# A weight conversion's shifted word in PSUM, and the conversions placed 300 instead of 1000 priorities late

## The chip, the core and the metric

The kernel runs on one core of a Trainium2 chip. The metric is the device time of one execution, in microseconds; lower is better. Engines are named TensorE (PE, with its weight loads PEld), VectorE (DVE), ScalarE (ACT), GpSimd (POOL) and SyncE (SP, whose queue issues the DMAs).

## What is computed

Attention with a top-32 mask (4 batches, 8 heads, 576 tokens, head size 64), then a feed-forward net on the 2304 tokens, then a mixture of 8 experts of which each token takes 2.

```
scores = q @ k.T / sqrt(D);  keep the 32 largest of each row;  attn = softmax;  x = attn @ v
h = maximum(x @ w_in, 0);  x = (h * h) @ w_out            # 512 -> 2048 -> 512
top2 of x @ w_gate + log1p(exp(x @ w_noise)) * noise       # routing
out[token] += weight * (maximum(x @ w1[e], 0) @ w2[e])     # 512 -> 1024 -> 512, per expert
```

The FFN's weights can arrive as 64-bit floats. They are turned into two 32-bit parts on the chip (a rounded high part and the rest), so that products can be made of three TensorE passes: high by high, high by low, low by high.

## The kernel before

Attention goes in 80 units: a unit is a pair of heads of one batch for 128 query rows, or the pair's last 64 rows. A full unit has two searches of 128x576 scores, a unit of last rows one, 144 in all. A search runs on VectorE (`scores`, lines 351 to 384): in six segments of 96 the 8 largest are taken and struck out (L367, L368), the 8 largest of what is left are taken over the row (L369, once per search, so its count shows the progress), and four more rounds run over the candidates (L372, L374). Then `softmax` (L386 to L397) works on ScalarE and GpSimd, TensorE transposes (`transpose4`, `rest`) and multiplies with V (`times_v`), and `finish` splits the result into the FFN's input xT.

The first batch's 16 units (12 full ones and 4 of last rows, 28 searches) hold the three token tiles of FFN chunk 0. The loop over the units (L731 to L762) emits the scores of a unit two units ahead (`AHEAD`). The FFN (`ffn`, L265) works on chunks of three tiles of 128 tokens and 16 slices f of its weights. For each slice, 12 matmuls into a tile `pf` (L286 to L288), ScalarE and GpSimd steps on it, and 9 matmuls (L272 to L274) into three accumulators `acc`, which are held from the first slice of a chunk to its last. The accumulators come from the pool `ps_acc`, three PSUM banks. The FFN's pieces are emitted between attention's, as filling work, through `step`.

The order on every engine is set by a planner: it takes the instructions by priority (a higher number is later, and each instruction emitted adds to it) among those that are ready in its own model of time, and within an engine the order it finds is fixed. `FILL_LATER = 350` gives the FFN's filling work a priority 350 later than where it is emitted; `side` (L640) does the same for the conversions and for the zero fill of the output buffers (`ZEROS_LATER = 1500`). Two conversions are emitted at the end of each unit until all 32 are out, that is by the end of the 16th unit. A tile is taken from its pool in the order in which the tiles are asked for, so the conversions stand ahead of the FFN.

One conversion (`convert`, L140) loads 512 KB (`raw`, three buffers), and on words of 128x512: ScalarE scales the high words into `ca` (L148), VectorE shifts `ca` by three bits (L149) and combines it with the sign bit of the high words (L150), ScalarE scales the low words (L151), GpSimd adds (L152), ScalarE rounds to the high part (L155), GpSimd subtracts (L156), and SP stores the two parts to `wsc` in DRAM (L157), from where the FFN loads them. The PSUM has 8 banks: `pf` 1, `acc` 3, the scores 2, attention's other tiles 2.

Of the kernel before, what the change touches and what calls it, by code (L numbers as in the profile page):

```python
# [8 lines left out]
F32 = mybir.dt.float32  # L9
F32R = mybir.dt.float32r  # L10
I32 = mybir.dt.int32
U32 = mybir.dt.uint32
BF16 = mybir.dt.bfloat16
AF = mybir.ActivationFunctionType
ALU = mybir.AluOpType
PSUM = bass.MemoryType.PSUM

P = 128
# [16 lines left out]
EARLY = 2  # L35
SOON = 300
FILL_LATER = 350
CONVERT_LATER = 1000
ZEROS_LATER = 1500


# [11 lines left out]
def attention_ffn_moe(ctx: ExitStack, tc: tile.TileContext, q, k, v, w_ffn, w_route, noise, w_exp, out,  # L53
# [3 lines left out]
    nc = tc.nc  # L57
    B, H, S, D = SHAPE
    NT, DM = out.shape
# [44 lines left out]
    for t, (b, i) in enumerate(tiles):  # L104
        if i == 0:
            nc.gpsimd.iota(tok_i[:, t:t + NFULL], pattern=[[P, NFULL]], base=b * S, channel_multiplier=1)
        elif i is None:
            nc.gpsimd.iota(tok_i[:, t:t + 1], pattern=[[0, 1]], base=b * S + NFULL * P, channel_multiplier=1)
            nc.gpsimd.tensor_scalar(tok_i[LEFT:P, t:t + 1], tok_i[LEFT:P, t:t + 1], 1.0, float(S - LEFT),
                                    op0=ALU.mult, op1=ALU.add)  # L110
# [7 lines left out]
    ps_acc = wctx.enter_context(tc.tile_pool(name="ps_acc", bufs=3, space=PSUM))  # L118
# [21 lines left out]
    def convert(vpool, f, which):  # L140
        n = DM
        raw = vpool.tile([P, 2 * n], U32, name="raw", bufs=3 if keep is not None else 2)
        nc.sync.dma_start(raw, w_ffn[f, which])
        pair = raw.rearrange("p (j t) -> p j t", t=2)
        lo_w, hi_w = pair[:, :, 0], pair[:, :, 1]
        a = vpool.tile([P, n], U32, name="ca", bufs=2)

        nc.scalar.activation(a.bitcast(F32), hi_w.bitcast(F32), AF.Copy, scale=2.0 ** -112)  # L148
        nc.vector.tensor_scalar(a, a, 3, None, op0=ALU.logical_shift_left)  # L149
        nc.vector.scalar_tensor_tensor(a, hi_w, 0x80000000, a, op0=ALU.bitwise_and, op1=ALU.bitwise_or)  # L150
        nc.scalar.activation(lo_w, lo_w, AF.Copy, scale=2.0 ** -29)  # L151
        nc.gpsimd.tensor_tensor(a, a, lo_w, op=ALU.add)  # L152
        val = a.bitcast(F32)
        sp = vpool.tile([P, 2, n], F32R, name="csp", bufs=2 if keep is not None else 1)
        nc.scalar.activation(sp[:, 0, :], val, AF.Copy)  # L155
        nc.gpsimd.tensor_tensor(sp[:, 1, :], val, sp[:, 0, :].bitcast(F32), op=ALU.subtract)  # L156
        nc.sync.dma_start(wsc[f][:, which], sp.bitcast(F32))  # L157
# [482 lines left out]
    def side(work, n, offset):  # L640
        at = tc.cur_priority
        tc.cur_priority = at + offset
        for _ in range(n):
            next(work, None)
        tc.cur_priority = at
# [4 lines left out]
    def conversions():  # L650
        for f in range(NF):
            for which in range(2):
                convert(vpool, f, which)
                yield
# [76 lines left out]
    for i in range(NU):  # L731
        credit = rate(i)

        def fill(part):
            step(credit * part)
# [24 lines left out]
        fill(FILLS[7])  # L760
        side(convs, CONVERTS, CONVERT_LATER)
        side(zeros, 1, ZEROS_LATER)  # L762
# [34 lines left out]
    for e in range(E):  # L797
        nc.vector.tensor_scalar(over[:, e:e + 1], base[:, e:e + 1], float(-(e * NT + CAP)), 0.0,
                                op0=ALU.add, op1=ALU.max)
# [180 lines left out]
```

## Time and profile before

| | us |
|---|---|
| median of 3 runs (1410.55 to 1411.21) | 1410.84 |
| the profiled execution | 1400.43 |
| its span | 1398.7 |
| TensorE busy in it | 1256.0 |
| VectorE busy in it | 954.0 |
| ScalarE busy in it | 842.5 |
| GpSimd busy in it | 798.0 |

The rows below come from that one profiled execution. Times are microseconds from the start of its span unless a column says ns. A busy share is the time in which an engine worked on an instruction; an instruction that stands and waits for a resource of the memory inside the engine counts as busy.

### The profile page before, as it was taken

Reading aid. Unit: us, or ns where it says so; the run is one execution under the profiler, and the core shown is the slowest. Engines: PE = TensorE matmul, PEld = TensorE weight load, DVE = VectorE, ACT = ScalarE, POOL = GpSimd, SP = SyncE. Lnnn points to the kernel's source line nnn. Section 1 sums busy time; section 2 is a strip of 40 time slices with the busy share of each in tenths; the row PEclk is TensorE's granted clock in tenths of the full one; section 3 lists DMA queues with packets and bytes.
Section 4 is the critical chain, followed back from the end, with each engine's and each line's share of the span. In section 5 each row is a group of like instructions: output and inputs, shape, how many; then the busy total and the mean of one; then the engine's idle time right before and its main releaser. Section 6 shows DMA issues by size and latency. Waiting matters only on the chain.

```text
span 1398.7 us, 26415 instructions
## 1 busy us (share of the span) xinstructions
PE 1256.0 (90%) x7937; PEld 1084.3 (78%) x7937; DVE 954.0 (68%) x5089; ACT 842.5 (60%) x1741; POOL 798.0 (57%) x1366
## 2 busy tenths in 40 slices
PE   2576659998999999999999999899899999999996
PEld 1354447877788888878878888788788999989995
DVE  8999999999989998899998001145554434444342
ACT  5768778978888787888878434354443333233321
POOL 4869898996888675868748523605233405134131
PEclk9877559999999999999999999999999999999998
DMA  9984557973367445546514776737664335444241
GB/s 332 350 306 151 181 179 244 343 235 116 133 207 243 146 141 188 178 144 202 182 65 153 246 248 211 265 106 235 200 210 142 130 114 165 125 143 134 91 145 38
DMA packets 85241, 257.50 MB, mean 184 GB/s; under 512 B 10716, under 2 KB 10844, under 8 KB 85088
## 3 DMA queue, kind: packets, MB, share of 16 engines
q1 hardware_dynamic: 75808, 227.32, 49.0%
q0 software_dynamic: 9280, 28.40, 5.6%
q8 instruction: 65, 1.06, 0.3%
q14 instruction: 88, 0.72, 0.1%
HBM read 205.71 MB, written 52.06 MB: 184 GB/s over the span
## 4 chain that ended last, share of the span: by engine, by line
PE 50%; DVE 31%; DMA 6%; ACT 5%; POOL 4%; issue 3%; SPq 0%; POOLq 0%; DVEq 0%; ACTq 0%
DVE w L368 9%; DVE m L367 6%; PE ph L573 5%; PE ph L572 5%; PE ph L574 5%; PE acc L555 5%; PE acc L553 5%; PE acc L554 5%; DVE m L369 4%; DVE cand L374 4%; DVE m L372 3%; PE acc L274 2%; PE acc L272 2%; PE acc L273 2%; PE pa L445 2%
## 5 line engine op out<-in xcount | busy, mean ns | idle before, releaser
L395 POOL TENSOR_TENSOR sb<-sb,w 128x576 f32<-128x576 f32 x144 | 207.4, 1445 | 16.5 <-ACT w L394 14.7
L368 DVE MATCH_REPLACE8 w<-m,sb 128x96 f32<-128x96 f32 x864 | 201.4, 242 | 0.0
L579 DVE SCALAR_TENSOR_TENSOR ht<-ph,ht 128x384 fp32r<-128x384 f32 (+1 forms) x128 | 62.7, 490 | 183.5 <-ACT ht L578 183.2
L578 ACT ACTIVATE ht<-ph 128x384 fp32r<-128x384 f32 (+1 forms) x128 | 55.9, 437 | 218.4 <-PE ph L574 218.3
L594 POOL DMA_INDIRECT out<-y,info x40 | 44.9, 1122 | 244.3 <-DVE y L593 237.4
L367 DVE MAX8 m<-sb 128x8 f32<-128x96 f32 x864 | 168.2, 244 | 16.4 <-ACT sb L359 14.8
L356 PE MATMUL ps<-K,qt 128*128 128x288 f32 x640 | 135.3, 336 | 39.4 <-POOL K L324 15.8
L572 PE MATMUL ph<-xe,wi 128*128 128x384 f32 (+1 forms) x512 | 159.9, 312 | 2.1 <-DVE xe L524 1.9
L573 PE MATMUL ph<-xe,wi 128*128 128x384 f32 (+1 forms) x512 | 159.9, 312 | 0.8 <-DVE xe L524 0.8
L574 PE MATMUL ph<-xe,wi 128*128 128x384 f32 (+1 forms) x512 | 159.6, 312 | 0.2 <-DVE wi L566 0.2
L356 PEld LDWEIGHTS ps<-K,qt 128*128 128x128 f32 x640 | 106.4, 212 | 52.1 <-ACT sb L359 17.5
L296 POOL TENSOR_TENSOR gt<-r,gt 128x384 fp32r<-128x384 f32 x96 | 97.6, 1017 | 67.0 <-ACT gt L295 62.4
L553 PE MATMUL acc<-wo,ht 128*128 128x512 f32 x320 | 126.8, 399 | 1.0 <-DVE y L593 1.0
L396 ACT ACTIVATE sb<-sb,keep 128x576 f32<-128x576 f32 x144 | 112.0, 778 | 23.6 <-POOL sb L395 23.1
L408 PE MATMUL pa<-ident,sb 128*128 128x128 f32 x576 | 98.8, 297 | 30.0 <-ACT sb L396 15.7
L554 PE MATMUL acc<-wo,ht 128*128 128x512 f32 x320 | 125.5, 395 | 0.0
L394 ACT ACTIVATE w<-sb,keep 128x576 f32<-128x576 f32 x144 | 110.6, 774 | 21.8 <-POOL keep L390 21.4
L286 PE MATMUL pf<-xT,wi 128*128 128x384 f32 x320 | 112.1, 350 | 6.8 <-ACT r L292 4.0
L272 PE MATMUL acc<-wo,gt 128*128 128x512 f32 x288 | 113.5, 404 | 2.5 <-DMA wo<-wsc 1.6
L287 PE MATMUL pf<-xT,wi 128*128 128x384 f32 x320 | 109.3, 341 | 4.8 <-POOL xT L423 4.8
L408 PEld LDWEIGHTS pa<-ident,sb 128*128 128x128 f32 x576 | 67.8, 148 | 55.8 <-ACT sb L396 18.1
L273 PE MATMUL acc<-wo,gt 128*128 128x512 f32 x288 | 110.7, 395 | 0.0
(181 smaller groups left out, 3528.3 us busy)
## 6 DMA issues: line engine op xcount, KB each, us to landing
wi<-wsc SPq DMA_DIRECT2D x96, 512.0 KB, 4.5
wo<-wsc SPq DMA_DIRECT2D x96, 512.0 KB, 4.5
raww<-in_exp SPq DMA_DIRECT2D x80, 512.0 KB, 3.8
raw<-in_ffn SPq DMA_DIRECT2D x32, 512.0 KB, 4.3
wsc<-csp SPq DMA_DIRECT2D x32, 512.0 KB, 4.2
xs<-xr SPq DMA_DIRECT2D x40, 258.0 KB, 7.5
mr<-xs SPq DMA_DIRECT2D x40, 258.0 KB, 3.2
qn<-in_q SPq DMA_DIRECT2D x40, 256.0 KB, 3.0
```

Source lines behind the costliest of these rows:

```text
L272: nc.tensor.matmul(acc[tt], gt[:, 0, sl], wo[:, 0, :], start=(f == 0), stop=False)
L273: nc.tensor.matmul(acc[tt], gt[:, 0, sl], wo[:, 1, :], start=False, stop=False)
L356: nc.tensor.matmul(ps[:, n, 0:HS], st, kt[:, n * HS:(n + 1) * HS], start=(i == 0), stop=(i == len(pairs) - 1))
L367: nc.vector.max(top, sb[:, sl])
L368: nc.vector.match_replace(out=w[:, sl], in_to_replace=top, in_values=sb[:, sl], imm_value=NEG)
L395: nc.gpsimd.tensor_tensor(sb, sb, w, op=ALU.subtract)
L408: nc.tensor.transpose(pt[:, c * P:(c + 1) * P], e[:, c * P:(c + 1) * P], ident)
L553: nc.tensor.matmul(acc[t], hs[i][:, 0, sl], wo[:, 0, :], start=(f == 0), stop=False)
L554: nc.tensor.matmul(acc[t], hs[i][:, 0, sl], wo[:, 1, :], start=False, stop=False)
L572: nc.tensor.matmul(ph[:, 0:n], wi[:, 0, sl], xe[i][:, 0, c, :], start=(c == 0), stop=False)
L573: nc.tensor.matmul(ph[:, 0:n], wi[:, 0, sl], xe[i][:, 1, c, :], start=False, stop=False)
L574: nc.tensor.matmul(ph[:, 0:n], wi[:, 1, sl], xe[i][:, 0, c, :], start=False, stop=(c == NC - 1))
```

## The change

The scaled high word is written to a PSUM tile of the pool `ps_acc`, under the name of the FFN's accumulators. VectorE shifts it there, and the combining step reads it from there and writes `ca` in SBUF. The number of instructions and the shapes stay. The offset of the conversions' priorities goes from 1000 to 300, which is less than the FFN's 350.

```diff
-CONVERT_LATER = 1000
+CONVERT_LATER = 300
...
-        nc.scalar.activation(a.bitcast(F32), hi_w.bitcast(F32), AF.Copy, scale=2.0 ** -112)
-        nc.vector.tensor_scalar(a, a, 3, None, op0=ALU.logical_shift_left)
-        nc.vector.scalar_tensor_tensor(a, hi_w, 0x80000000, a, op0=ALU.bitwise_and, op1=ALU.bitwise_or)
+        high = ps_acc.tile([P, DM], F32, name="acc")
+        nc.scalar.activation(high, hi_w.bitcast(F32), AF.Copy, scale=2.0 ** -112)
+        high = high.bitcast(U32)
+        nc.vector.tensor_scalar(high, high, 3, None, op0=ALU.logical_shift_left)
+        nc.vector.scalar_tensor_tensor(a, hi_w, 0x80000000, high, op0=ALU.bitwise_and, op1=ALU.bitwise_or)
```

## Rows read from the trace of the kernel before

**Rows 1.** The page, busy time of each engine: us, share of the span, instructions.
```profile
PE 1256.0 (90%) x7937; PEld 1084.3 (78%) x7937; DVE 954.0 (68%) x5089; ACT 842.5 (60%) x1741; POOL 798.0 (57%) x1366
```
**Rows 2.** Stretches of the span: length, busy time of each engine, granted clock, DMA share.
```profile
core 0: us, PE busy (x) PEld busy (x) DVE busy (x) ACT busy (x) POOL busy (x), PEclk, DMA share, GB/s
0.00:100.00 100.00, 50.54 (x286) 38.41 (x286) 92.03 (x542) 64.72 (x120) 63.12 (x100) 0.88 0.98 338
100.00:216.00 116.00, 70.68 (x416) 53.64 (x416) 109.84 (x651) 91.51 (x180) 106.10 (x126) 0.65 0.50 171
216.00:327.00 111.00, 101.35 (x672) 85.00 (x672) 108.72 (x640) 94.33 (x204) 99.07 (x129) 1.00 0.78 266
327.00:380.00 53.00, 47.97 (x385) 40.74 (x385) 52.48 (x374) 47.34 (x102) 40.31 (x76) 0.97 0.32 108
380.00:700.00 320.00, 316.13 (x2281) 273.90 (x2277) 295.06 (x2011) 261.57 (x567) 244.42 (x415) 1.00 0.55 181
```
**Rows 3.** The chain that ended last, from 0 to 420 us, its shares by line.
```profile
by line: DVE w L368 18.8%; DVE m L367 10.2%; DVE m L369 8.1%; DVE cand L374 6.6%; DVE m L372 5.9%; DVE ca L150 5.7%; issue 4.3%; DVE ca L149 3.4%; DMA raw<-in_ffn 3.0%; PE ps L356 2.6%; DMA kn<-in_k 2.5%; PE pa L445 2.4%; POOL K L324 1.9%; 
```
**Rows 4.** Lines 149 and 150: ns min/median/max, first and last start in us.
```profile
L149 DVE TENSOR_SCALAR ca<-ca x32: 397/576/4482, 19.1 to 296.5; 128x512 uint32<-128x512 uint32 x32
L150 DVE SCALAR_TENSOR_TENSOR ca<-raw,ca x32: 664/808/2697, 22.1 to 297.8; 128x512 uint32<-128x512 uint32 x32
```
**Rows 5.** Timeline of VectorE and GpSimd at the two longest steps: start, duration in us.
```profile
223.58 4.48 DVE L149 TENSOR_SCALAR ca<-ca 128x512 uint32<-128x512 uint32 x1
...
220.57 0.48 POOL L423 TENSOR_TENSOR xT<-x,xT 128x128 fp32r<-128x128 f32 x1
...
226.71 1.06 POOL L296 TENSOR_TENSOR gt<-r,gt 128x384 fp32r<-128x384 f32 x1
230.11 1.30 POOL L152 TENSOR_TENSOR ca<-ca,raw 128x512 uint32<-128x512 uint32 x1 [2.34 <-issue]
...
57.04 2.70 DVE L150 SCALAR_TENSOR_TENSOR ca<-raw,ca 128x512 uint32<-128x512 uint32 x1
...
56.55 2.64 POOL L324 TENSOR_TENSOR K<-kn,K 64x1152 fp32r<-64x1152 f32 x1 [2.06 <-DVE m L369]
```
**Rows 6.** Stretches, line 149 alone (first two) and line 150 alone (last two).
```profile
0.00:216.00 216.00, 17.00 (x22) 0.76 0.73 248
216.00:310.00 94.00, 12.10 (x10) 1.00 0.82 281
...
0.00:216.00 216.00, 23.94 (x22) 0.76 0.73 248
216.00:310.00 94.00, 11.06 (x10) 1.00 0.82 281
```
**Rows 7.** Groups by line: VectorE reading 128x512 of PSUM; busy us, mean ns.
```profile
L593 DVE SCALAR_TENSOR_TENSOR y<-acc,info,cur 128x512 f32<-128x512 f32 x40 | 28.2, 744 | 19.6 <-DMA out<-y,info 15.8 <-PE acc L555 3.7
L524 DVE TENSOR_TENSOR xe<-ph,xe 128x512 fp32r<-128x512 f32 x40 | 27.5, 689 | 25.5 <-ACT xe L523 25.5
```
**Rows 8.** Stretches, line 369 alone: one instruction per search.
```profile
0.00:216.00 216.00, 26.88 (x36) 0.76 0.73 248
216.00:310.00 94.00, 12.68 (x17) 1.00 0.82 281
310.00:380.00 70.00, 11.23 (x15) 0.98 0.38 126
```
**Rows 9.** Timeline of TensorE where chunk 0 takes its accumulators.
```profile
216.38 0.39 PE L272 MATMUL acc<-wo,gt 128*128 128x512 f32 x1
...
217.79 0.42 PE L286 MATMUL pf<-xT,wi 128*128 128x384 f32 x1
...
219.81 0.34 PE L288 MATMUL pf<-xT,wi 128*128 128x384 f32 x1
```
**Rows 10.** Stretches, GpSimd's lines 152 (first) and 156 alone.
```profile
216.00:310.00 94.00, 14.38 (x11) 1.00 0.82 281
...
216.00:310.00 94.00, 16.08 (x12) 1.00 0.82 281
```
**Rows 11.** DMA issues of raw weights, 0 to 100 and 100 to 216 us: median us.
```profile
raw<-in_ffn SPq DMA_DIRECT2D x9, 512.0 KB, 7.6
...
raw<-in_ffn SPq DMA_DIRECT2D x15, 512.0 KB, 3.5
```

## What the change does to the time: the prediction

> **What bounds the kernel now.** I read three views first. The busy shares say that TensorE, at 90%, is the fullest engine over the whole span, with VectorE at 68% [rows 1]; an average over stages, so I cut the span at the places where the FFN starts and where its first chunk ends [rows 2]. Up to 216 us TensorE is half empty (121.2 of 216 us) while VectorE is at 109.8 of the 116 us that precede the start, and GpSimd at 106.1. From 216 to 380 us VectorE is full (161.2 of 164 us) and TensorE nearly (149.3). From 380 to 700 us TensorE is busy for 316.1 of 320 us, and after 900 us the experts keep it full too. So the time is set by two things: how late TensorE gets its first FFN work, and how much it idles between 216 and 380 us, which is 9.65 + 5.03 = 14.7 us. The chain of waits agrees: up to 420 us nearly all its large shares are VectorE's search, and the two VectorE steps of the weight conversion (lines 149 and 150) hold 9.1% of it, 38 us [rows 3]. A gain after 380 us is not to be had from this change; the conversions are over by then.
>
> **What the conversions cost on VectorE.** There are 32. The shift (line 149) takes 0.40 us at its shortest, 0.58 at the median and 4.48 at its longest; the combining step (line 150) 0.66, 0.81 and 2.70 [rows 4]. Nothing in the data differs between them. What differs is GpSimd: the longest shift starts at 223.58 and ends at 228.06 us, and GpSimd has instructions back to back from 220.57 to 227.77, then a gap until 230.11; the longest combining step (57.04 to 59.74) covers GpSimd's L324 (56.55 to 59.19) [rows 5]. So the two engines exclude each other for these forms, and VectorE waits with its queue behind it. The sums are 29.1 and 35.0 us; 17.0 + 23.9 = 40.9 us fall before 216 us (22 conversions) and 23.2 us after (10) [rows 6].
> The Trainium skill says the same in "SBUF — State Buffer", section "Who interferes with whom": a VectorE instruction that uses both port pairs, or has two SBUF inputs against a GpSimd read, excludes GpSimd for its whole length, and one with at most one SBUF input does not. By that rule both waits go with this change, and the trace agrees as far as the waits that it shows.
>
> **Part 1: the shifted word in PSUM.** Removed: the shift on SBUF, and a combining step with two SBUF inputs. Added: a shift whose input and output are in PSUM, and a combining step with one input in PSUM and one in SBUF. No row shows that shift. The nearest rows of VectorE reading 128x512 from PSUM are L524 (0.689 us, the other input in SBUF) and L593 (0.744 us, three operands) [rows 7]; neither of them is stretched as the conversion steps are, though GpSimd works there as well. I take 0.69 for the shift and 0.74 for the combining step: 1.43 x 32 = 45.8 us in place of 64.1, 18.3 us less. The bounds: as fast as today's shortest combining step, 0.66 + 0.66 = 1.32, saves 21.9 us; both at 0.744 saves 16.5; and if the waits stay whatever the memory, the shift goes from 0.40 to 0.69 and VectorE has 0.29 x 32 = 9.3 us more.
> A rule that speaks against the change stands in the Trainium skill, "VectorE: DVE Perf Modes", section "Why PSUM operands drop a tier": a 4-byte operand in PSUM loses the doubled rate that a one-input step has in SBUF. The unhindered 0.40 us against 0.69 is in line with it; taken alone it makes the change a loss of those 9.3 us, and it is the waits, which it doesn't speak of, that decide.
> The ScalarE step that writes the word (line 148) keeps its count and about its 0.67 us; ScalarE is busy for 91.5 of the 116 us before the FFN [rows 2], so a tenth of a microsecond each is hidden. The SBUF buffer "ca" is now taken by the combining step instead of by ScalarE, which shortens how long it is held. I cost that at nothing: in the conversion's chain GpSimd and the loads are later.
>
> **Part 2: 300 priorities late instead of 1000.** The planner's order is what moves; every step of a conversion moves with it: the load and the store on SP's queue, three ScalarE steps, two on VectorE, two on GpSimd. Where do they go? A head's search (one L369 each) counts the progress: 36 by 216 us, 17 from 216 to 310, 15 from 310 to 380 [rows 8]. The last pair is emitted in the 16th unit; those units hold 28 searches and the emission runs two units ahead, so some 32 are emitted by then. In fact the last combining step starts at 297.8 us [rows 4], with some 51 searches done: 19 searches for 1000 priorities, so about 6 for 300, and the last conversion should stand near the 38th search. That is two searches after 216 us, at 70/15 = 4.7 us each, plus the conversion work that has come forward, 45.8 - 40.9 = 4.9 us: about 230 us (an estimate). So VectorE is loaded by 5 us more ahead of that point, and by 23.2 us less from 216 to 310 us.
>
> **The wait that the change adds.** The PSUM tiles come from the FFN's three accumulators, so the first chunk can take its accumulators only when the last conversions have let go of theirs. Behind the first accumulating matmul in TensorE's queue stands everything that was ordered after it, attention's matmuls too, so the planner must place it late. In the trace that matmul runs at 216.38 us [rows 9]. At 230 us it is 14 us late. What that costs TensorE: the spacing of the accumulating matmuls is (217.79 - 216.38)/6 = 0.235 us and of the first layer's (219.81 - 217.79)/11 = 0.184 [rows 9]; a chunk has 16 x 9 of the one and 16 x 12 of the other, 33.8 + 35.3 = 69.1 us, in the 111 us from 216 to 327: 0.62 us of FFN work for each us. 14 x 0.62 = 8.7 us are put off, less the 12 matmuls of the second slice that can run ahead (2.2 us): 6.5 us lost.
>
> **What the freed VectorE gives back.** From 216 us on the search is 23.2 us shorter, so the second chunk's tokens are ready some 23 us sooner, and TensorE need not run dry at the end of the first chunk (the 5.03 us in 327 to 380) nor wait for the search before it (9.65). What it keeps is the idle share of 380 to 700 us, 1.2% of 164 = 2.0 us: 14.7 - 2.0 = 12.7 us gained. The rest of the VectorE time has no use, since TensorE is late next.
>
> **The sum.** -12.7 + 6.5 = -6.2 us; with the rounding of the estimates I say -6.5. The profiled execution took 1400.43 us, of which 1398.7 is the span, and so goes to 1394; it lies 10.4 us below the median of the runs shown, 1410.84, and the forecast for that is 1410.84 - 6.5 = 1404.3 us.
>
> **Rivals.** (a) *The whole VectorE saving counts.* If the gate costs nothing, because the planner gets the conversions done by 216 us, and the earlier FFN start holds too, 18.3 us are saved (21.9 at the lower bound): 1392.5, at least 1389. For it: the chain holds 38 us of conversion. Against it: TensorE has only 14.7 us to give after 216 us.
> (b) *GpSimd takes VectorE's place.* The conversions that come forward bring 14.4 + 16.1 = 30.5 us of GpSimd [rows 10]. Ahead of 216 us it has 36.9 us free in the first 100 and 9.9 in the next 116 [rows 2]. In the first 100 us the DMA engines are full (0.98) and a raw load lands in 7.6 us against 3.5 later [rows 2, 11], so conversions can hardly be hurried there. If none is, 30.5 - 9.9 = 20.6 us of GpSimd work push the gate from 216 to some 237 us: 20.6 x 0.62 = 12.8 us lost, 12.7 gained, no change: 1411.
> (c) *Slower: the accumulators are held too long.* The decisive point is that same 237 us for the last combining step; beyond it each us costs 0.62. If the loads and GpSimd hold the conversions to 250 us, TensorE loses 34 x 0.62 - 2.2 = 18.9 us: +6 us, 1417; at the old pace (298 us) it would lose 50.8 - 2.2, and end near 1447. For it: raw loads land late just when they would be wanted sooner. Against: after 100 us the DMA engines are half free (0.50).
> (d) *The change doesn't do what it says.* The waits stay with PSUM operands: VectorE has 9.3 us more, all in stages where it is full, and the gate on top: 1411 + 9.3 - 5, about 1415. Against it: the unstretched rows with a PSUM input.
>
> **How the numbers follow.** The forecast has 0.45, (a) 0.20, (b) 0.14, (c) 0.15, (d) 0.06. From 0.2% (2.8 us) on a measurement of this kernel can tell a change. Faster: the forecast and (a), 0.65. Same: (b), 0.14. Slower: (c) and (d), 0.21. The range leaves out the far ends of (a) and (c): 1391 to 1417.
>
> **What would show it.** Right: the shift and the combining step between 0.6 and 0.8 us each with no long ones; 45 us in all; the last combining step before 237 us; TensorE over 97% busy from the FFN's start to 380 us. Step by step: an uneven shift says that (d) holds; GpSimd full and VectorE with gaps from 100 us on says (b); the first accumulating matmul waiting behind a conversion, or standing well after 237 us, says (c). The forecast is wrong above all if the planner's new order does not keep the search at its pace while three engines take conversions twice as densely.

## The result, and the profile after

The changed kernel takes 1417.78 us (median of 5 runs, 1416.56 to 1420.54), the kernel before beside it 1410.6: a ratio of 1.0062, 95% interval 1.0038 to 1.0085. In a later group of runs it was 1.0105 (1.0083 to 1.0126). It is slower, where the forecast said 6.5 us faster. The kernel before itself had medians of 1408.2, 1400.1, 1400.6 and 1410.8 us in the four groups of experiments (a group is timed side by side), so times are compared within a group only, and ratios across groups with care. The two traced executions, 1400.43 us before and 1420.54 after, lie further apart than the medians do. A second trace of the changed kernel (1413.10 us) has its first accumulating matmul at 239.64 us and its last combining step at 249.56, as the first has them.

VectorE's two conversion steps and ScalarE's write, which are the conversions' instructions that write the PSUM tile or read it (ns min/median/max, first and last start in us), in the changed kernel:

```profile
L149 ACT ACTIVATE acc<-raw x32: 614/640/664, 15.4 to 237.6; 128x512 f32<-128x512 f32 x32
L151 DVE TENSOR_SCALAR acc<-acc x32: 671/686/700, 17.2 to 241.3; 128x512 uint32<-128x512 uint32 x32
L152 DVE SCALAR_TENSOR_TENSOR ca<-raw,acc x32: 658/675/691, 19.6 to 249.1; 128x512 uint32<-128x512 uint32 x32
```

These answer [rows 4]. The long ones are gone: the shift went from 397 to 4482 ns to 671 to 700, the combining step from 664 to 2697 to 658 to 691. All 32 of both cost 22.0 + 21.6 = 43.6 us in place of 64.1. The change does to VectorE what it was costed at. And the last combining step starts at 249.1 us instead of 297.8.

The same stretches as in [rows 2] (length, busy time of each engine, granted clock, DMA share):

```profile
0.00:100.00 100.00, 53.23 (x268) 39.99 (x268) 84.46 (x532) 66.20 (x122) 65.54 (x103) 0.88 0.99 342
100.00:216.00 116.00, 73.08 (x417) 53.45 (x418) 105.30 (x620) 93.48 (x185) 104.18 (x129) 0.67 0.61 208
216.00:327.00 111.00, 101.16 (x648) 87.00 (x648) 100.56 (x681) 87.58 (x191) 85.93 (x123) 0.93 0.61 207
327.00:380.00 53.00, 49.24 (x401) 40.79 (x401) 50.92 (x365) 46.14 (x102) 39.01 (x62) 1.00 0.35 115
380.00:700.00 320.00, 311.02 (x2210) 266.80 (x2211) 287.94 (x1944) 255.91 (x548) 237.52 (x412) 0.99 0.53 177
```

Two things are to be seen. TensorE's idle time from 216 to 380 us is 164 - 150.4 = 13.6 us, where 14.7 were before and 2.0 were forecast, and it has done this at a granted clock of 0.93 instead of 1.00 in the first of the two stretches. And VectorE is idle for 26.2 of the first 216 us, against 14.1 before, and for 12.5 of the 164 us up to 380, against 2.8: it did not put its saving into the search. Line 371 alone, one instruction per search, answers [rows 8]:

```profile
0.00:216.00 216.00, 25.35 (x34) 0.77 0.78 270
216.00:310.00 94.00, 14.31 (x19) 0.91 0.64 217
310.00:380.00 70.00, 11.26 (x15) 1.00 0.38 125
```

34 searches by 216 us where 36 were done before, and by 380 us 68 in each. So attention is two searches late at first and then where it was; what stays late is the FFN. The timeline where chunk 0 takes its accumulators, which answers [rows 9] (start, duration in us, and in brackets the idle time before with what ended it; TensorE, then VectorE's last combining step, then TensorE):

```profile
234.90 0.66 PE L410 MATMUL pa<-ident,sb 128*128 128x128 f32 x4 [2.73 <-DVE x L419]
...
238.85 0.80 PE L274 MATMUL acc<-wo,gt 128*128 128x512 f32 x1
...
243.58 0.39 PE L274 MATMUL acc<-wo,gt 128*128 128x512 f32 x1
...
249.09 0.68 DVE L152 SCALAR_TENSOR_TENSOR ca<-raw,acc 128x512 uint32<-128x512 uint32 x1
...
249.82 0.50 PE L274 MATMUL acc<-wo,gt 128*128 128x512 f32 x1
...
257.70 0.79 PE L274 MATMUL acc<-wo,gt 128*128 128x512 f32 x1 [3.11 <-DMA wo<-wsc]
```

The first accumulating matmul is at 238.85 us, 22.5 us later than before. It writes the first of the three accumulators, all of which were begun by 217.31 in the kernel before. The second is first written at 243.58, and the third at 249.82, 0.05 us after the last combining step has ended (249.09 + 0.68 = 249.77). Only then can the second layer's weights of the first slice be let go, and the next load of them lands so late that TensorE stands another 3.11 us, up to 257.70. By 260 us the FFN has begun 60 first-layer and 24 accumulating matmuls, where the kernel before had begun 96 and 54; with 0.184 and 0.235 us each that is 16.7 against 30.4 us of work.

In the same stretch TensorE's granted clock falls. Stretches of 10 us from 230 us on, TensorE alone (busy time, granted clock, DMA share), first the changed kernel, then the one before:

```profile
230.00:240.00 10.00, 6.76 (x45) 0.80 0.85 317
240.00:250.00 10.00, 9.17 (x62) 0.86 0.12 39
250.00:260.00 10.00, 6.69 (x42) 0.82 0.95 328
260.00:270.00 10.00, 10.00 (x43) 0.83 0.64 197
```
```profile
230.00:240.00 10.00, 8.87 (x59) 1.00 0.66 220
240.00:250.00 10.00, 9.20 (x64) 1.00 0.95 279
250.00:260.00 10.00, 9.72 (x70) 1.00 1.04 401
260.00:270.00 10.00, 8.86 (x64) 1.00 0.99 348
```

The clock has two levels, 1.2 and 2.4 GHz (0.5 and 1.0 here), and the lower one is granted twice here: it begins 1.1 us after TensorE has stood idle for 2.73 us (up to 234.90, for attention's step on VectorE), and again within the idle 3.11 us up to 257.70:

```profile
236.00:242.80 6.80, 6.29 (x31) 0.50 0.45 180
256.50:263.30 6.80, 5.60 (x14) 0.50 0.55 210
```

The kernel before has 1.00 in both stretches, so a "busy" TensorE hides part of the loss. In the second trace of the changed kernel the lower level lasts half as long, 3.4 us twice. (The counts of matmuls don't compare: from 260 to 270 us 42 of the changed kernel's 43 are the FFN's long ones, of the other's 64 only 26.)

### The profile page after: what moved, and what is told of

Its sections match the earlier page's. It is cut to its first block, busy times and chain, and to the rows that moved or that the text cites. A ratio compares the mean times of both kernels' runs of the same rounds, so it can differ in the third digit from the quotient of the medians.

```text
span 1418.8 us, 26461 instructions
## 1 busy us (share of the span) xinstructions
PE 1274.9 (90%) x7937; PEld 1095.1 (77%) x7937; DVE 936.1 (66%) x5089; ACT 844.5 (60%) x1741; POOL 793.8 (56%) x1366
## 4 chain that ended last, share of the span: by engine, by line
PE 59%; DVE 17%; DMA 9%; ACT 6%; POOL 5%; issue 3%; SPq 0%; another core or an unknown queue 0%; POOLq 0%; DVEq 0%; ACTq 0%
DVE w L370 5%; PE ph L575 5%; PE ph L574 5%; PE ph L576 5%; PE acc L557 4%; PE acc L555 4%; PE acc L556 4%; PE pa L447 4%; PE acc L274 4%; PE acc L275 3%; PE acc L276 3%; DVE m L369 3%; PE ps L358 3%; PE pf L288 3%; PE pf L290 2%
## 5 line engine op out<-in xcount | busy, mean ns | idle before, releaser
L397 POOL TENSOR_TENSOR sb<-sb,w 128x576 f32<-128x576 f32 x144 | 204.4, 1426 | 27.8 <-ACT w L396 26.6
L358 PE MATMUL ps<-K,qt 128*128 128x288 f32 x640 | 139.9, 345 | 39.3 <-ACT sb L361 15.0
L410 PE MATMUL pa<-ident,sb 128*128 128x128 f32 x576 | 101.8, 301 | 29.1 <-ACT sb L398 15.0
```

The costliest lines, as they stand in the source:

```text
L358: nc.tensor.matmul(ps[:, n, 0:HS], st, kt[:, n * HS:(n + 1) * HS], start=(i == 0), stop=(i == len(pairs) - 1))
L397: nc.gpsimd.tensor_tensor(sb, sb, w, op=ALU.subtract)
L410: nc.tensor.transpose(pt[:, c * P:(c + 1) * P], e[:, c * P:(c + 1) * P], ident)
```

## The experiments

A theory here is one reading of the loss, and each run was chosen to part two of them. Theory 1: the loss is the wait for the accumulators, which the last conversions hold. Theory 2: it is the conversions that come forward and crowd attention out, through the offset. The theories A (VectorE's time sets when the FFN starts), B (GpSimd's does; one expectation calls it theory 3) and D (the full DMA engines of the first 100 us hold the conversions) are about the gain that was missing. The order that the planner makes for each engine already says something: the offset moves little in it. For the kernel before, the planned program is the same with 900, 990 or 1100 as with 1000; with 300 the last combining step stands behind the 50th search as before, and in the changed kernel behind the 41st with 300 and the 42nd with 1000, as the traces show too.

**The offset alone.** The kernel before with

```diff
-CONVERT_LATER = 1000
+CONVERT_LATER = 300
```

> The kernel before with the offset of 300 alone; the shifted word stays in SBUF. Theory 1 (the accumulators are the cause, the offset is not): no accumulator is taken by a conversion, chunk 0's first accumulating matmul stays near 216 us, the time stays within 3 us of the kernel before. Theory 2 (conversions crowded into the first 216 us slow attention): the last conversion comes forward by some 50 us and the time rises by about the 7 us of the changed kernel.

Measured: 1412.99 us, ratio 1.0027 (1.0002 to 1.0051). Line 150 in it:

```profile
L150 DVE SCALAR_TENSOR_TENSOR ca<-raw,ca x32: 669/1064/3005, 19.7 to 294.8; 128x512 uint32<-128x512 uint32 x32
```

The conversions stay where they were (297.8 before, 294.8 here) and keep their long waits, and the first accumulating matmul runs at 209.3 us. The offset brings no conversion forward, so theory 2 can't rest on it. But the time is 4.8 us above the kernel before by the medians, where at most 3 were expected, although the FFN starts 7 us sooner: the offset alone has a price, and its cause stays open.

**The PSUM tile alone.** The changed kernel with

```diff
-CONVERT_LATER = 300
+CONVERT_LATER = 1000
```

> The changed kernel with the offset put back to 1000; the shifted word in PSUM alone. Theory 1: the first accumulating matmul stays near 239 us and the time is that of the changed kernel, 1415 to 1420. Theory 2: the last conversion goes back to near 298 us; without crowding the time falls to that of the kernel before or under it (1400 to 1411), unless the gate then costs far more (0.62 us for each us beyond 237: above 1440).

Measured: 1412.96 us, ratio 1.0041 (1.0020 to 1.0063).

```profile
L152 DVE SCALAR_TENSOR_TENSOR ca<-raw,acc x32: 666/674/689, 21.6 to 246.8; 128x512 uint32<-128x512 uint32 x32
```

The last combining step is at 246.8 us and the first accumulating matmul at 237.2, both as in the changed kernel. The time is 2 us under the range expected. So it is the PSUM tile that brings the conversions forward, and with it the whole wait; the offset is not needed for either. The ratios of the two halves, 1.0027 and 1.0041, multiply to 1.0068, near the whole change's 1.0062; and the offset alone, without the wait, is no faster in this group than the tile alone with it (1412.99 and 1412.96 us). The likely reason, argued and not tested by itself: "ca" has two buffers, and since ScalarE no longer takes one at the start of a conversion, the planner can start the next sooner.

**The wait alone.** Offset 300, and

```diff
         nc.vector.scalar_tensor_tensor(a, hi_w, 0x80000000, a, op0=ALU.bitwise_and, op1=ALU.bitwise_or)
+        held = ps_acc.tile([P, DM], F32, name="acc")
+        nc.vector.tensor_copy(held[:, 0:1], a[:, 0:1].bitcast(F32))
```

> The wait alone: offset 300, the shift in SBUF as before, but each conversion also takes an accumulator and has one column copied into it after the combining step (32 copies of 128x1 on VectorE, some 2 us in all), and nothing reads it. Theory 1: the first accumulating matmul stands behind the last conversion, near 300 us or later; each us beyond 216 takes up to 0.62 us from TensorE, so 80 to 110 us of delay cost 40 to 60 us: 1450 to 1470. Theory 2: the gate costs little, since attention runs ahead meanwhile: under 1425.

Measured: 1449.17 us, ratio 1.0288 (1.0263 to 1.0313), 41 us over the kernel before in the same group. TensorE's timeline, with what ended its idle time:

```profile
294.22 0.48 PE L274 MATMUL acc<-wo,gt 128*128 128x512 f32 x1
...
295.75 0.50 PE L274 MATMUL acc<-wo,gt 128*128 128x512 f32 x1 [0.58 <-DVE acc L152]
```

The second accumulator is taken as soon as the copy into the one held before is done. Against the kernel with the offset alone, which differs in the held accumulators and the 32 copies (0.14 us each), the wait of 294.2 - 209.3 = 84.9 us costs 1449.17 - 1412.99 = 36.2, that is 0.43 us for each us (0.53 against the kernel before). The time is 1 us under the range expected. Attention does not run ahead meanwhile: 63 searches are done by 380 us, 66 with the offset alone.

**Twenty shifts in PSUM, twelve in SBUF.** Offset 1000, and

```diff
+        if 2 * f + which < 20:
+            high = ps_acc.tile([P, DM], F32, name="acc")
...
+        else:
+            nc.scalar.activation(a.bitcast(F32), hi_w.bitcast(F32), AF.Copy, scale=2.0 ** -112)
...
```

> Offset 1000; the first 20 conversions shift in PSUM, the last 12 in SBUF as before, so the last to hold an accumulator is over before chunk 0 wants it. Theory 1: no gate, first accumulating matmul near 216 us; VectorE saves 20 x 0.64 = 13 us in the first 216 us, and if the search is what holds up chunk 0 the time falls to 1400 to 1406. Theory 3 (GpSimd, full in the same stretch, takes its place): the time stays within 3 us of the kernel before though the gate is gone.

Measured: 1401.42 us, ratio 0.9971 (0.9947 to 0.9996). The first accumulating matmul is at 209.7 us: no wait, and a gain of 7 us by the medians, 4 by the ratio.

**Undoing one thing.** In the changed kernel only the last four conversions go back to SBUF (`< 28` in place of `< 20`, offset 300), run beside the changed kernel itself and the one with 20:

> The changed kernel as it is, beside the next three on one chip, for a second trace of it. Theory 1: first accumulating matmul near 239 us again, 1415 to 1420 us.

> The changed kernel with one thing undone: the last 4 of the 32 conversions shift in SBUF as before; 28 stay in PSUM, the offset stays at 300. Theory 1 (the accumulators held by the last conversions are the loss): first accumulating matmul near 212 us instead of 239, and 8 to 13 us less than the changed kernel on the same chip. Theory 2 (conversions that come forward, or slow PSUM steps): within 3 us of the changed kernel.

> The kernel with 20 shifts in PSUM and offset 1000 again, beside the changed one and the one with 28. Theory A: 1398 to 1405 us, under the kernel before by 2 to 9 us. Rival: its gain over the kernel before was that of one chip; within 3 us of the kernel before.

Measured beside each other: the changed kernel 1414.64 us (1.0105), with 28 in PSUM 1398.99 (0.9985, interval 0.9969 to 1.0000), with 20 in PSUM 1395.51 (0.9961, 0.9947 to 0.9974). Four conversions of 32 are worth 15.65 us, some more than expected. The second trace of the changed kernel shows the wait by name, though little of it as idle time there, since the planner has put other work before it:

```profile
250.28 0.50 PE L274 MATMUL acc<-wo,gt 128*128 128x512 f32 x1 [0.32 <-DVE ca L152]
```

and with 28 in PSUM the first accumulating matmul (line 279) is at 219.2 us, 20.4 us before the changed kernel's 239.6 in the same group, though the last of the conversions that hold an accumulator combines at 230.0:

```profile
L279 PE MATMUL acc<-wo,gt x76: 387/393/500, 219.2 to 419.9; 128*128 128x512 f32 x76
...
L153 DVE SCALAR_TENSOR_TENSOR ca<-raw,acc x28: 657/672/689, 19.6 to 230.0; 128x512 uint32<-128x512 uint32 x28
```

This is the clearest run for theory 1: the rest of the change stays, nearly as many conversions come forward (26 by 216 us, 27 in the changed kernel), and the loss is gone; crowding ahead of the FFN, theory 2, is not what costs. What else moves is the end: the last conversion, now in SBUF, combines at 264.1 us instead of 249.6. The start of 219.2 us is later than the 212 that I expected.

**Twenty-eight with offset 1000,** in another group:

> Offset 1000; 28 conversions shift in PSUM, the last 4 in SBUF. VectorE saves 28 x 0.64 = 18 us instead of 13. Theory 1 with A: only the last few conversions make the wait for the accumulators, so the first accumulating matmul stays before 222 us and the time is that of the kernel with 20 or some us less, 1397 to 1402. Rival: the 28th lets go of its accumulator only after 225 us, the wait comes back and the time is 1405 or more.

Measured: 1405.71 us, ratio 1.0041 (1.0027 to 1.0054), first accumulating matmul at 211.6 us. The wait is gone, as expected, but the gain is not there: slower than the kernel before in that group, by 5.6 us. In the same group a kernel that holds all 32 (below, with offset 300) had 1417.35, which is 11.6 us more. But all 32 with offset 1000 had the same ratio of 1.0041 in its own group, with the wait; at that offset no two runs made side by side show what undoing the last four is worth.

**More VectorE work.** As with twenty, and

```diff
             nc.vector.tensor_scalar(high, high, 3, None, op0=ALU.logical_shift_left)
+            nc.vector.tensor_scalar(high, high, 0, None, op0=ALU.logical_shift_left)
```

> As the kernel with 20 shifts in PSUM and offset 1000, but each of these 20 conversions shifts twice (the second time by zero bits): 20 x 0.68 = 13.7 us more on VectorE, nearly all ahead of 216 us, nothing more elsewhere. Theory A (what that kernel gained is VectorE's time): the 7 us go again, 1405 to 1412. Theory B (GpSimd is what holds up the stretch, the gain came from its waits): the time stays within 3 us of 1401.4.

Measured: 1416.25 us, ratio 1.0118 (1.0101 to 1.0134). The first accumulating matmul, line 280 here and line 279 in the kernel with twenty of another group:

```profile
L280 PE MATMUL acc<-wo,gt x75: 387/393/709, 230.0 to 418.1; 128*128 128x512 f32 x75
```
```profile
L279 PE MATMUL acc<-wo,gt x78: 387/395/628, 209.8 to 416.5; 128*128 128x512 f32 x78
```

13.7 us of VectorE put the FFN's start off by 20 us, and the time is above the range expected. Theory A holds in this direction: added VectorE time costs at least in full.

**GpSimd's work given to VectorE.** As with twenty, and

```diff
-        nc.gpsimd.tensor_tensor(sp[:, 1, :], val, sp[:, 0, :].bitcast(F32), op=ALU.subtract)
+        nc.vector.tensor_tensor(sp[:, 1, :], val, sp[:, 0, :].bitcast(F32), op=ALU.subtract)
```

> As the kernel with 20 shifts in PSUM and offset 1000, but the last subtraction of every conversion runs on VectorE instead of GpSimd: GpSimd 32 x 1.28 = 41 us less, VectorE 32 x 0.69 = 22 us more, with two inputs in SBUF. Theory A (VectorE holds up the stretch): slower by 5 to 12 us than 1401.4. Theory B (GpSimd does): faster by 3 to 10 us.

Measured: 1423.13 us, ratio 1.0159 (1.0142 to 1.0176), first accumulating matmul at 237.9 us. GpSimd was busy for 143.5 of the first 216 us, where the kernel before has 169.2 [rows 2], and it was no help. So GpSimd alone does not set the start, and theory B falls in that form. But the subtraction took 34.5 us on VectorE where 22 were expected (0.66 to 3.09 us each), more than the 13.7 us that cost 20 us above; what less GpSimd work would give with VectorE left as it is was not tried.

**The zero fill later, first attempt.** The changed kernel, and

```diff
-        side(zeros, 1, ZEROS_LATER)
+        if i >= 14:
+            side(zeros, 2, ZEROS_LATER)
```

> The changed kernel, with the zero fill of the output buffers (15 MB of stores) emitted from the 15th unit on, two pieces for each unit, instead of one from the first unit on. Theory D (full DMA engines in the first 100 us are why the conversions end late): raw loads land in under 5 us there instead of 7.6, more than 9 conversions are done by 100 us instead of 7, the first accumulating matmul comes forward from 239 to 225 to 232 us, and the time falls by 0.5 to 0.6 us for each of these, to 1409 to 1414. Rival (the planned order holds them): 7 conversions by 100 us, the time stays at 1415 to 1420.

Measured: 1417.35 us, ratio 1.0117 (1.0099 to 1.0135). All 58 stores of the fill still go in the first 100 us (here the 40 of one buffer; issues, size, us to landing):

```profile
xs<-xr SPq DMA_DIRECT2D x40, 258.0 KB, 7.5
```

The planner took them early anyway. The run says nothing on theory D.

**The zero fill later, by data.** Two kernels, the changed one and the one with twenty, each with

```diff
+        nc.gpsimd.tensor_scalar(fill[:, 0:1], dsts[0][:, 0, 1, P:P + 1].bitcast(F32), 0.0, 0.0, op0=ALU.mult, op1=ALU.add)
...
-        side(zeros, 1, ZEROS_LATER)
+        if i >= 8:
+            side(zeros, 2, ZEROS_LATER)
```

> The changed kernel; the zero fill's source tile gets one column from xT of the 7th unit times zero, so that none of its 58 stores can go before about 90 us. Theory D (full DMA engines hold the early conversions and idle VectorE): at least 12 conversions by 100 us instead of 7, raw loads land in under 5 us there, the last conversion and the first accumulating matmul come forward from 239 to 225 to 235 us, and the time is 4 to 10 us under that of the changed kernel. Rival: the stores are as much in the way after 90 us, or VectorE and GpSimd are the bound: first accumulating matmul at 236 us or later, time within 4 us of the changed kernel's ratio of 1.006 to 1.0105.

> The kernel with 20 shifts in PSUM and offset 1000, with the same hold on the zero fill. Theory D: conversions done earlier leave VectorE to the search after 100 us, and TensorE idles less between 216 and 380 us; first accumulating matmul before 210 us, ratio to the kernel before 0.990 to 0.995. Rival: conversions brought forward take VectorE's time from the search, so chunk 0 is ready later, after 214 us; ratio 0.997 or more.

Measured: 1422.38 us, ratio 1.0079 (1.0051 to 1.0107), and 1398.22 us, ratio 0.9909 (0.9884 to 0.9934). Now no store of the fill goes in the first 100 us, 16 raw loads are issued there (9 in [rows 11]), and 14 and 13 conversions have combined by 100 us instead of 7. But VectorE is no fuller (82.9 and 84.1 of the first 100 us), 14 searches are done instead of 16 or 17, and the first accumulating matmul stays at 237.0 and 212.3 us. So theory D's first half holds (the DMA engines held the conversions) and its second doesn't: the FFN starts no sooner, since, as the counts suggest, what the conversions gain the search loses. With all 32 in PSUM the wait stands where it stood. By its ratio the kernel with twenty is the fastest of the study nevertheless, 12.6 us under the kernel before in its group. Why it gains that much with the same FFN start isn't settled.

**Conversions spread out.** As with twenty, but 18 in PSUM and

```diff
-        side(convs, CONVERTS, CONVERT_LATER)
+        side(convs, 1 + (i % 4 == 0), CONVERT_LATER)
```

> 18 shifts in PSUM, offset 1000, and conversions emitted 5 in four units instead of 8, so that more of them come after the FFN has started. Theory A (VectorE's work ahead of the FFN's start sets that start): two to four conversions fewer ahead of 216 us, 3 to 7 us of VectorE, first accumulating matmul before 209 us, time 2 to 5 us under the kernel with 20. Rival (attention needs the VectorE time after 216 us as much): the same time as that kernel within 3 us.

Measured: 1405.19 us, ratio 1.0033 (1.0022 to 1.0044). The planner put off only one conversion (24 by 216 us, 25 with twenty), the last to 276.0 us from 265.7; the first accumulating matmul came at 219.9 us instead of 209.8, and the time rose by 9.7 us. So the edit failed at what it was for. The start was late here without any accumulator being held, and cost 0.96 us for each us.

## Why the prediction was wrong

Two terms of its sum failed: the gain, forecast at 12.7 us and measured at 1.6, and the wait, forecast at 6.5 us and measured at 15.65.

**What bounds the kernel: right.** VectorE before the FFN starts, then TensorE. 13.7 us more of VectorE cost 20 us of start, and the ratio went from 0.9961 to 1.0118. Whether GpSimd is a second bound close behind stays open.

**VectorE's conversion steps: right.** 1.43 us for each pair was forecast, 1.36 measured, 45.8 against 43.6 us. That GpSimd's exclusion was the cause of the long ones is borne out: in both kernels GpSimd works on the same forms throughout, and the steps with one SBUF input or none vary by 33 ns at most. The kernel with twenty has both kinds in one trace (lines 152 and 153 in PSUM, 156 and 157 in SBUF; its second trace):

```profile
L152 DVE TENSOR_SCALAR acc<-acc x20: 672/686/698, 19.1 to 165.8; 128x512 uint32<-128x512 uint32 x20
L153 DVE SCALAR_TENSOR_TENSOR ca<-raw,acc x20: 662/672/697, 22.4 to 169.5; 128x512 uint32<-128x512 uint32 x20
L156 DVE TENSOR_SCALAR ca<-ca x12: 411/922/2739, 177.8 to 264.2; 128x512 uint32<-128x512 uint32 x12
L157 DVE SCALAR_TENSOR_TENSOR ca<-raw,ca x12: 667/1318/2779, 180.1 to 265.7; 128x512 uint32<-128x512 uint32 x12
```

**Where the conversions go: wrong in the reason, short in the place.** I read 19 searches for 1000 priorities out of one point and scaled it to 300. The offset brings no conversion forward; the PSUM tile does. The prediction had seen that "ca" is held for less time with it and put that at nothing, since GpSimd and the loads are later in the chain; with the tile alone the last combining step came from 297.8 to 246.8 us. The last conversion was put at the 38th search and 230 us; it combined at 249.1 us, with 41 searches done. No row of the trace before could have said so; the planned order could.

**The wait: right in kind, too short, its price not settled.** Forecast 14 us late for 6.5 us, at 0.62 us for each us. Measured 22.5 us late for the first accumulator and 32.5 for the third (249.82 against 217.31), and 15.65 us for undoing it. Where two kernels run side by side differ in which conversions hold an accumulator, the one with the later start is slower each time, but not at one price. For each us of start it is 0.37 (28 against 20), 0.42 (all 32 against 20 with offset 1000), 0.43 (the held accumulators and their copies), (1414.64 - 1395.51)/(239.6 - 209.8) = 0.64 (the changed kernel against 20), 0.77 (32 against 28) and (1422.38 - 1398.22)/(237.0 - 212.3) = 0.98 (32 against 20 with the late zero fill). The forecast's 0.62 lies in the middle of that, which does not show it right: it counts FFN work put off, and not the lower clock that came with TensorE's idle time, nor what else changes between two orders.

**The gain: wrong in size.** This is the term that fails worst. 12.7 us were to come back from TensorE's idle time between 216 and 380 us, since the search would be 23 us shorter there. Without the wait, the change yields 1.6 us (28 in PSUM, ratio 0.9985), 5.1 to 6.8 us (20 in PSUM), or in one group a loss of 5.6 us (28 with offset 1000). TensorE's idle time in that stretch is 164 - 104.09 - 49.21 = 10.7 us with 28 in PSUM, so 4.0 us of it came back:

```profile
216.00:327.00 111.00, 104.09 (x712) 90.05 (x712) 108.53 (x691) 92.97 (x203) 90.86 (x131) 1.00 0.70 232
327.00:380.00 53.00, 49.21 (x372) 41.37 (x369) 51.62 (x353) 43.81 (x98) 37.28 (x68) 0.99 0.39 122
```

There 67 searches are done by 380 us, and 68 in the changed kernel and in the kernel before: the search is sooner in neither. The saving was not passed on. In the changed kernel's first 216 us VectorE's conversions took 19.3 + 18.2 = 37.5 us instead of 40.9, but 27 were done instead of 22, and VectorE stood idle 12 us longer. The shift has 4.1 us of that (6.2 us of waits for ScalarE's scaled word, which itself stood 9.6 us for raw loads, against 2.1 before); attention's own steps have the rest, 6.1 us at x for TensorE (1.1 before) and 4.0 for GpSimd's sb (0.4 before). I had taken a fuller VectorE queue for a shorter one: in these traces the work brought forward met data that wasn't there yet. The sum of -12.7 + 6.5 became -1.6 + 15.65 = 14.1 us in the group that has both; how the 7.2 us of the first result divide was not measured.

**The rivals.** (c) described what happened, with its deciding point: at 237 us the gain and the wait were to balance, and a last conversion at 250 us was to give 1417. It combined at 249.1 us and the time was 1417.8. The place is right (that the loads and GpSimd hold it there, as (c) has it, is shown in part, by the 9.6 us that ScalarE stood for raw loads); the two terms behind it were each sized wrong, the gain too large and the wait too small, so the agreement of the total is partly luck. (b) named the obstacle (full DMA engines, 7 conversions in the first 100 us) and was right that they can't be hurried there (7 again in the changed kernel, 14 once the zero fill is held back), but GpSimd as the bound is not borne out. (a) and (d) are out; the 5 us that (d)'s sum takes off come from no row. I gave (c) 0.15; the row that should have raised it was [rows 11] together with [rows 6]: with 9 loads issued and 7 conversions combined in the first 100 us, 25 were left for the 116 us in which VectorE and GpSimd are nearly full [rows 2].

**What stays open.** The same first accumulating matmul does not give the same time: the offset alone starts the FFN at 209.3 us and is slower than the kernel with 20 in PSUM that starts at 209.7, by 11.6 us by the medians in one group. The planned orders behind that point differ, and I have not traced which differences matter. So an order by itself can move the time by nearly as much as the 15.65 us of the wait; it is the agreement of the pairs above, and the run in which little but the held accumulators differs, that make the wait the cause. Differences of half a per cent between two orders should be read as such.

## What to carry to other kernels

A borrowed buffer is free only until its owner's first use: look at who asks for it next, when the last borrower lets go, and what stands behind that wait on the owner's engine, and leave the last few borrowers out (here 4 of 32 were worth 15.65 us). Time saved on a full engine counts only if the engine has something ready to do with it; count what is moved forward against the loads that feed it. And an offset in a planner's priorities is not a delay: look at the planned order before reasoning from it.

## What the runs showed of the hardware

ScalarE wrote the word to PSUM in 640 ns (median) where it took 670 to SBUF. VectorE's shift with both sides in PSUM takes 671 to 700 ns; with both in SBUF it takes 404 to 419 where GpSimd is idle all through it, and up to 4482 beside GpSimd: the slower form is the better one here because it is steady (22.0 us for all 32 against 29.1). One shift in SBUF (223.58 to 228.06 us) outlasted five GpSimd instructions in a row and ended 0.29 us after the last of them [rows 5]. TensorE's idle time was paid twice in the changed kernel: beside idle stretches of 2.73 and 3.11 us the granted clock stood at 0.50 for 6.8 us each (3.4 in its second trace), and the accumulating matmuls in there took 0.63 us instead of 0.39.
